# DeltaNet and a SiLU feed-forward in one kernel: where the vector engine makes the weight sums for the last chunk

## The chip, the cores and the metric

The kernel runs on one core of a Trainium2 chip. A core has five engines with a queue each: TensorE (PE in the profile; its weight loads are listed as PEld), VectorE (DVE), ScalarE (ACT), GpSimd (POOL) and SyncE (SP), which here issues DMAs. Each engine works through its own list of instructions in order, and waits on semaphores for the others. Matrix products land in PSUM; ACT and DVE read them from there. The metric is the device time of one execution in microseconds (us), as the median of several.

## What is computed

A DeltaNet layer runs over 4 batches x 8 heads of 768 tokens with 48 features, token by token; its output goes through a feed-forward layer.

```python
for t in range(S):                       # S = 768, state is (B, H, 48, 48)
    y[:, :, t] = einsum('bhd,bhde->bhe', q[:, :, t], state)
    v_old = einsum('bhde,bhd->bhe', state, kt)          # kt: key, normalised
    state = state + bt * einsum('bhd,bhe->bhde', kt, vt - v_old)
x = y.transpose(0, 2, 1, 3).reshape(3072, 384)
h = x @ w_in                             # 384 -> 2048
g = h * sigmoid(h)
out = g @ w_out                          # 2048 -> 384
```

## The kernel before

The 768 tokens are cut into six chunks of 128 (`NCH` = 6), numbered 0 to 5. Inside a chunk the recurrence becomes triangular systems, solved by merging inverted blocks of 32 into 64, and by two halves of 64 tokens (`hf`) that follow one another through the state. Two groups of batches (`g`) go side by side. For a chunk `c`, `solve(c)` is a generator whose steps are, in order: first merge (`merge(c, g, False)`), keys of the first half (`keys(c, g, 0)`), second merge (`merge(c, g, True)`), inner products and old state of the first half (`inner` into `pz`, `old` into `pyc`), state update and new outputs (`made`: `update` into `pu`, `new`), copies (`copy_out`), keys of the second half, inner products of the second half, then its outputs.

`keys` matters here. PE multiplies keys with the state (line 893, into `ph`), and DVE then adds `ph` to the values `vf` (line 898). `inner` (line 905) is PE's next use of that `vf`. Each engine's list is in the order in which the program writes it, since `pin` ties every instruction behind the one before it on its engine. So a DVE instruction that is written earlier stands in front of the `vf` add in DVE's queue, whatever PE waits for.

The feed-forward of an earlier chunk runs between the steps of the solve: the outer loop calls `go(solving)` for one step of the solve and `run(n)` for `n` pieces of the feed-forward. While chunk 5 is solved, the pieces are those of chunk 4: its second layer, `combine(4, hf)`, whose products go to `px` and `py` (line 1451), whose sums of activations are made on DVE (`sum_g`, line 1428), and whose results ACT copies out of PSUM (`kept`, line 1459) for DVE to add to `o` (line 1462).

The first layer for the last chunk, `hidden_by_chains(5)`, runs after that, with fewer products and more sums. It takes combinations of the blocks of `w_in` as weights, which `sum_weights()` makes on DVE: eighteen instructions over 128 x 512 elements, in tiles that the profile calls `w_in`, `sums_of_w_in` and `kb` (lines 1285 and 1280). `weight_sums` is that generator, and `go(weight_sums, n)` writes its next `n` instructions. `BY_CHAINS` is `(5,)`, so this happens only in the loop's pass for chunk 5.

Of the kernel before, what the change touches and what calls it, by code (L numbers as in the profile page):

```python
# [19 lines left out]
def kernel(  # L20
# [85 lines left out]
    def go(steps, n=1):  # L106
        for _ in range(n):
            next(steps, None)

    def together(*parts):  # L110
        for _ in zip_longest(*parts):
            pass
# [82 lines left out]
    def in_blocks(c):  # L195

        return 1 < c < NCH
# [446 lines left out]
    def block_in(c, by_scalar=False):  # L644
        there, g, _ = blocks[c]
        issue(g, there[:], by_scalar)
# [242 lines left out]
    def keys(c, g, hf):  # L889

        ph = bank(CC, "ph")
        for u, p, e, n, of, _ in of_heads():
            yield pin(nc.tensor.matmul(  # L893
                ph[on(e, hf, g), n * D : (n + 1) * D], lhsT=kqs[c, g * HB + u][of, p, 0, on(e, hf, g)],
                rhs=states[g][of, u, p, 0:D], start=True, stop=True,
            ))
        to = vfs[c][:, hf, g * HB : (g + 1) * HB]
        pin(nc.vector.tensor_tensor(out=to, in0=to, in1=by_heads(ph), op=ALU.add))

    def inner(c, g, hf, room=CC):  # L900

        pz = bank(room, "pz")
        for u, p, e, n, _, _ in of_heads():
            rows = on(e, hf, g)
            yield pin(nc.tensor.matmul(  # L905
                pz[rows, n * D : (n + 1) * D], lhsT=xis[g][rows, u * H + 2 * p + e, :],
                rhs=vfs[c][rows, hf, g * HB + u, p, :], start=True, stop=True,
            ))
        to = z_of(g)[:, :, hf]
        if c == 0 and hf == 0:  # L910
            by = (by_act, by_dve) if g == 0 else (by_dve, by_act)
            at = slab[:, g * HB * NP * 2 * D + D :][:, 0 : HB * NP * 2 * D]
            by[0](at.rearrange("p (n w) -> p n w", w=2 * D)[:, :, 0:D], pz[:, 0:DM].rearrange("p (n d) -> p n d", d=D))
            by[1](to, by_heads(pz))
        else:
            by_act(to, by_heads(pz))

    def update(c, g, hf):

        if c == NCH - 1 and hf == 1:  # L920
            return
        pu = bank(CC, "pu")
        for u, p, e, n, to, _ in of_heads():
            rows = on(e, hf, g)
            yield pin(nc.tensor.matmul(  # L925
                pu[to, n * D : (n + 1) * D], lhsT=by_pair(kbufs[c % 2], g)[rows, u, p, e],
                rhs=z_of(g)[rows, u, hf, p], start=True, stop=True,
            ))
        for e in range(2):
            of = slice(W * e, W * e + D)  # L930
            to = states[g][of]
            pin(nc.vector.tensor_tensor(out=to, in0=to, in1=by_heads(pu[of]), op=ALU.add))  # L932
# [7 lines left out]
    def first_outputs(g):  # L940

        pys = [bank(A, f"py{e}") for e in range(2)]
        for u in range(HB):
            for a in range(NKT):
                for n in range(2):
                    for half in range(2):
                        f = P * a + W * half
                        h = f // D + n
                        p, e = h // 2, h % 2
                        at = ((g * HB + u) * NP + p) * 2 * D + D + f - D * h  # L950
                        pin(nc.tensor.matmul(
                            pys[e][HALVES[half], C * a + W * u : C * a + W * (u + 1)],
                            lhsT=slab[on(e, 0, g), at : at + W], rhs=aps[0, g][1][on(e, 0, g), u, h, :],
                            start=True, stop=True,
                        ))
        xT, half = x_half(0, g, 0)
        to = xT[:, :, half]
        even, odd = (py[:, 0 : NKT * C].rearrange("p (a t) -> p a t", a=NKT) for py in pys)
        by_act(to, even)
        pin(nc.vector.tensor_tensor(out=to, in0=to, in1=odd, op=ALU.add))  # L960
# [3 lines left out]
    def move():  # L964
        for to, of in moves:
            in_line(nc.sync.dma_start(out=to, in_=of))
        moves.clear()

    def old(c, g, hf):

        py = pys[g] = bank(A, "pyc")
        for u, p, e, _, of, to in of_heads():
            yield pin(nc.tensor.matmul(  # L973
                py[to, C * p + W * u : C * p + W * (u + 1)],
                lhsT=states[g][of, u, p, 0:D], rhs=kqs[c, g * HB + u][of, p, 1, on(e, hf, g)],
                start=p == 0 and u == 0, stop=False, skip_group_check=True,
            ))
        if hf != g:
            by_act(read[0:D], py[0:D, 0 : 512 : W])
# [45 lines left out]
    def copy_out():  # L1025
        together(copies.pop(0))
# [14 lines left out]
    def solve(c):  # L1041

        if c == 0:
            together(inner(0, 0, 0, CC))
            together(inner(0, 1, 0, M))
            yield
            first_outputs(0)
            yield
            first_outputs(1)
            yield  # L1050
            together(update(0, 0, 0), update(0, 1, 0))
            yield
            together(keys(0, 0, 1), keys(0, 1, 1))
            yield
            together(inner(0, 0, 1), old(0, 0, 1))
            yield
            together(inner(0, 1, 1), old(0, 1, 1))
            yield
            together(update(0, 0, 1), update(0, 1, 1))
            yield  # L1060
            together(new(0, 0, 1), new(0, 1, 1))
            move()
            copy_out()
            copy_out()
            block_in(1, True)
            yield
            return
        together(merge(c, 0, False), merge(c, 1, False))
        if c > 1 and in_blocks(c + 1):
            load_blocks(k, c + 1, G0)  # L1070
        yield
        together(keys(c, 0, 0), keys(c, 1, 0))
        yield
        together(merge(c, 0, True), merge(c, 1, True))
        yield
        for hf in range(2):
            if hf == 1:
                together(keys(c, 0, 1), keys(c, 1, 1))
                if c > 1 and in_blocks(c + 1):
                    turn_all(c + 1, 0, G0)  # L1080
                    load_blocks(q, c + 1, G1)
                    turn_all(c + 1, 0, G1)
                yield
            for g in range(2):
                together(inner(c, g, hf), old(c, g, hf))
            if hf == 1 and c > 1 and in_blocks(c + 1):
                turn_all(c + 1, 1, G0)
            yield
            made(c, hf)
            yield  # L1090
            copy_out()
            if hf == 0:
                yield
# [145 lines left out]
    BY_CHAINS = (NCH - 1,)  # L1239
# [664 lines left out]
    weight_sums = sum_weights()  # L1904
# [44 lines left out]

    for c in range(2, NCH):  # L1950
        solving, more = solve(c), c + 1 < NCH
        for n in range(8):
            go(solving)
            run((1, 1, 2, 2, 1, 1, 2, 2)[n] if c == 2 else (2, 2, 2, 2, 1, 1, 2, 2)[n])
            if n == 2 and c > 2 and more:
                assert done[0] >= start(c) - OUTPUT - 4
                load_blocks(k, c + 1, G1)
            if n == 3 and c > 2 and more:
                load_blocks(q, c + 1, G0)
            if n > 0:  # L1960
                go(after, 8)
            if c in BY_CHAINS:
                go(weight_sums, 2)
        go(after, 99)
        go(solving)
        run()
        if c in BY_CHAINS:
            go(weight_sums, 99)
        assert next(solving, 0) == 0
        if c == 2:  # L1970
            pieces = chained(pieces, *(feed_forward(c) for c in range(2, NCH)))
        if not more:
            break
        run(1 if c == 2 else 2)
        step = block_steps(c + 1)
        ready = prepare(c + 1)
        go(ready)
        run()
        go(ready)
        go(sums_in)  # L1980
        go(sums_in)
        linked(load_v, c + 1)
        load_k(c + 2)
        run_to(start(c))
        paced(invert(c + 1, step), 7 if c == 2 else 4)
        after = lengths(c + 2) if c + 2 < NCH else iter(())
        run_to(start(c) + ITEMS + 3)
        for g in range(2):
            size(c + 1, g)
        for n in range(3 if c == 2 else 2):  # L1990
            go(after, 2 - n)
            run()
        go(after, 1)
# [31 lines left out]
```

## Time and profile before

| | us |
|---|---|
| median of 3 runs | 626.46 |
| the runs | 625.25, 626.46, 627.69 |
| the profiled execution | 627.13 |
| its span, first to last instruction | 625.4 |
| PE busy in it | 607.6 |
| DVE busy in it | 464.5 |
| PE idle at pz, waiting for DVE's add to vf | 1.27 |
| PE idle in its other waits for DVE | 1.2 (pl, line 798), 1.2 (px, line 871), 0.4 (pl, line 782), 0.2 (blocks) |

A row of the timeline has the start from the beginning of the span, the length, the engine, the line of the kernel, the operation, `out<-in` by the program's names, the shape, how many instructions of this kind ran in a row, and in brackets how long the engine was idle before them and which instruction ended the wait. Rows on one engine may overlap by some hundredths, since an instruction's end is recorded later than the next one's start. Rows with "q" behind the engine's name are its instruction queue. The windows view gives busy time by engine in a stretch, and the TensorE clock that was granted there as a share of the full one. Groups by line give busy time and, behind the comma, the mean in ns of one instruction.

### The profile page before, as it was taken

How to read it: one execution, taken by the hardware profiler on the slowest of the kernel's cores; microseconds unless marked ns; L12 is line 12 of the kernel's file. 1: busy time of each engine (PE TensorE's matmuls, PEld its weight loads, DVE VectorE, ACT ScalarE, POOL GpSimd, SP SyncE). 2: the span in 40 equal slices, each digit the busy share in tenths (PEclk: the TensorE clock that was granted, in tenths of full speed). 3: DMA queues.
4: the chain of work that ended last, by engine and by line, in shares of the span. 5: the costliest groups of instructions: out<-in, count | busy, mean ns of one | idle time of the engine just before them, and what ended most of it. 6: DMA issues, size and time to landing. Idle time of an engine off the chain costs nothing.

```text
span 625.4 us, 21910 instructions
## 1 busy us (share of the span) xinstructions
PE 607.6 (97%) x9554; PEld 532.3 (85%) x9554; DVE 464.5 (74%) x983; ACT 247.5 (40%) x562; POOL 82.2 (13%) x83
## 2 busy tenths in 40 slices
PE   8889899999999999999999999999999999999997
PEld 5688788666789988898898998899998899988997
DVE  5865688998978976779976868976869967544632
ACT  3566556142351133533424433424433414435310
POOL 5443620247000010000010000010000010000000
PEclk9959899999999999999999999999999999999999
DMA  7755654155425582236083445084351060110011
GB/s 154 179 120 167 200 135 109 51 153 125 107 54 124 99 146 51 64 81 120 0 155 87 101 93 106 2 155 105 88 103 39 1 112 17 39 25 1 2 25 26
DMA packets 143935, 55.06 MB, mean 88 GB/s; under 512 B 113488, under 2 KB 137296, under 8 KB 143840
## 3 DMA queue, kind: packets, MB, share of 16 engines
q1 hardware_dynamic: 143360, 53.00, 37.9%
q8 instruction: 75, 1.23, 0.8%
q10 hardware_dynamic: 480, 0.67, 0.4%
q14 instruction: 20, 0.16, 0.1%
HBM read 40.99 MB, written 10.49 MB: 82 GB/s over the span
## 4 chain that ended last, share of the span: by engine, by line
PE 53%; DVE 2%; DMA 1%; ACT 1%; issue 1%; SPq 0%; DVEq 0%; ACTq 0%
PE px L1451 12%; PE py L1451 10%; PE hu L1168 9%; PE hx L1168 8%; PE hx L1335 3%; PE hu L1335 3%; PE pa L585 2%; PE pz L905 1%; PE pyc L986 1%; PE pyc L973 1%; PE ph L893 1%; PE pu L925 1%; PE py L847 1%; DMA xe<-low 1%; PE px L847 1%
## 5 line engine op out<-in xcount | busy, mean ns | idle before, releaser
L1114 PE MATMUL phid<-xT,w_in 128*128 128x256 f32 x384 | 90.7, 390 | 0.0
L1114 PEld LDWEIGHTS phid<-xT,w_in 128*128 128x128 f32 x384 | 72.1, 193 | 10.6 <-issue 0.5
L1451 PE MATMUL py<-w_out,sums_of_g 128*128 128x192 f32 x320 | 57.3, 329 | 0.5 <-issue 0.5
L1451 PE MATMUL px<-sums_of_w,sums_of_g 128*128 128x192 f32 x320 | 57.2, 330 | 0.0
L1451 PEld LDWEIGHTS py<-w_out,sums_of_g 128*128 128x128 f32 x320 | 52.2, 190 | 1.2 <-issue 0.6
L1451 PEld LDWEIGHTS px<-sums_of_w,sums_of_g 128*128 128x128 f32 x320 | 52.1, 190 | 1.0 <-issue 0.5
L688 DVE SCALAR_TENSOR_TENSOR rank<-g,step,x 128x31 f32<-128x31 f32 (+15 forms) x124 | 49.7, 400 | 3.7 <-DMA g<-blocks 0.7
L693 DVE TENSOR_TENSOR x<-x,rank 128x31 f32<-128x31 f32 (+15 forms) x124 | 42.4, 342 | 4.4
L521 POOL TENSOR_TENSOR vf<-vf,n_slot 128x768 f32<-128x768 f32 x10 | 14.6, 1475 | 190.0 <-DVE sums_of_g L1428 146.9
L1428 DVE TENSOR_TENSOR sums_of_g<-gT 128x512 f32<-128x512 f32 (+2 forms) x44 | 27.7, 663 | 12.8 <-PE py L1451 12.5
L1462 DVE TENSOR_TENSOR o<-o,kept 128x192 f32<-128x192 f32 (+1 forms) x29 | 12.4, 426 | 33.0 <-ACT kept L1459 33.0
L1168 PE MATMUL hx<-xT,w_in 128*128 128x256 f32 x144 | 36.0, 379 | 0.0
L600 ACT COPY gT<-hu 128x512 f32<-128x512 f32 x36 | 21.1, 586 | 32.9 <-PE hu L1168 22.9
L1168 PE MATMUL hu<-xT,w_in 128*128 128x256 f32 x144 | 34.0, 379 | 0.0
L600 ACT COPY xT<-pyc 48x128 f32<-48x128 f32 (+2 forms) x120 | 31.2, 260 | 1.6
L932 DVE TENSOR_TENSOR state<-state,pu 48x384 f32<-48x384 f32 x44 | 24.3, 553 | 8.6 <-PE pu L925 7.5
L1168 PEld LDWEIGHTS hu<-xT,w_in 128*128 128x128 f32 x144 | 27.4, 190 | 3.7
L1168 PEld LDWEIGHTS hx<-xT,w_in 128*128 128x128 f32 x144 | 27.3, 190 | 3.6
L905 PEld LDWEIGHTS pz<-vf,xi 64*64 64x64 f32 x768 | 25.2, 142 | 4.5 <-issue 2.6
L1451 PE MATMUL py<-w_out,gT 128*128 128x192 f32 x160 | 29.0, 331 | 0.0
L1122 ACT ACTIVATE gT<-phid 128x512 f32<-128x512 f32 x24 | 14.4, 598 | 36.3 <-PE phid L1114 35.7
L1451 PE MATMUL px<-sums_of_w,gT 128*128 128x192 f32 x160 | 28.5, 329 | 0.0
(264 smaller groups left out, 1243.9 us busy)
## 6 DMA issues: line engine op xcount, KB each, us to landing
vf<-in_v_dram SPq DMA_DIRECT2D x48, 96.0 KB, 2.7
out_dram<-o SPq DMA_DIRECT2D x42, 96.0 KB, 2.2
w_out<-in_moe_w_in_dram SPq DMA_DIRECT2D x12, 256.0 KB, 3.0
sums_of_w<-in_moe_w_out_dram SPq DMA_DIRECT2D x8, 384.0 KB, 3.5
blocks<-ap SPq DMA_DIRECT2D x40, 64.0 KB, 2.0
g<-blocks SPq DMA_DIRECT2D x4, 512.0 KB, 3.5
up<-x SPq DMA_DIRECT2D x4, 512.0 KB, 3.1
xi<-up SPq DMA_DIRECT2D x16, 128.0 KB, 3.5
```

The costliest lines, as they stand in the source:

```text
L521: done = pin(nc.gpsimd.tensor_tensor(out=vf, in0=vf, in1=of, op=ALU.mult))
L600: return pin(nc.scalar.copy(to, of))
L688: pin(nc.vector.scalar_tensor_tensor(out=tv, in0=g[:, 0:m, m : m + 1].to_broadcast([P, m, n]), scalar=step[:, m : m + 1], in1=x[:, m : m + ...
L693: yield pin(nc.vector.tensor_tensor(out=x[:, 0:m, m:T], in0=x[:, 0:m, m:T], in1=tv, op=ALU.add))
L905: yield pin(nc.tensor.matmul(pz[rows, n * D : (n + 1) * D], lhsT=xis[g][rows, u * H + 2 * p + e, :], rhs=vfs[c][rows, hf, g * HB + u, p, : ...
L932: pin(nc.vector.tensor_tensor(out=to, in0=to, in1=by_heads(pu[of]), op=ALU.add))
L1114: pin(nc.tensor.matmul(ph[:, j * GT : (j + 1) * GT], lhsT=w_in[:, a, (2 * f + j) * P : (2 * f + j + 1) * P], rhs=xTs[c, hf][:, a, :], star ...
L1122: pin(nc.scalar.activation(out=hidden_of(c, hf, f), in_=ph[:], func=ACTF.Silu, scale=0.5))
L1168: pin(nc.tensor.matmul(to[:, GT * i : GT * (i + 1)], lhsT=weights[:, f], rhs=moving, start=start and i == 0, stop=True, skip_group_check=True,
L1335: pin(nc.tensor.matmul(to[:, GT * i : GT * (i + 1)], lhsT=weights[:, 2 * u + i], rhs=moving, start=start and i == 0, stop=True, skip_group ...
L1428: pin(nc.vector.tensor_tensor(out=sums_of_g[:, k, fs], in0=of[0], in1=of[1], op=op))
L1451: pin(nc.tensor.matmul(to, lhsT=at, rhs=quarter(f, *b) if isinstance(b, tuple) else sums_of_w[b][:, f], start=start and n == 0, stop=n == ...
```

## The change

The same eighteen instructions are written at three places instead of nine. Before: two behind each of the steps 0 to 7 of the loop (behind the solve's step, the feed-forward pieces and the other work of that step), and the rest at the end; with eighteen in all, two are left for the end. After: six ahead of step 0, four at the end of step 2, eight at the end of step 5.

```diff
     for c in range(2, NCH):
         solving, more = solve(c), c + 1 < NCH
+        if c in BY_CHAINS:
+            go(weight_sums, 6)
         for n in range(8):
             go(solving)
             run((1, 1, 2, 2, 1, 1, 2, 2)[n] if c == 2 else (2, 2, 2, 2, 1, 1, 2, 2)[n])
...
             if n > 0:
                 go(after, 8)
             if c in BY_CHAINS:
-                go(weight_sums, 2)
+                go(weight_sums, {2: 4, 5: 8}.get(n, 0))
         go(after, 99)
         go(solving)
         run()
-        if c in BY_CHAINS:
-            go(weight_sums, 99)
         assert next(solving, 0) == 0
         if c == 2:
             pieces = chained(pieces, *(feed_forward(c) for c in range(2, NCH)))
         if not more:
+            assert next(weight_sums, 0) == 0
             break
```

Only DVE's order changes; the lists of PE, ACT, POOL and SP are the same. Three pieces of DVE's list show it. The first is around chunk 5's first merge and first keys; `y` is the merge's copy out of PSUM, and the rows with `w_in` or `sums_of_w_in` as output are weight sums. Before:

```order
L1428 TENSOR_TENSOR sums_of_g<-sums_of_g,gT 128x512 x2
L603 COPY y<-py 32x512 x2
L1428 TENSOR_TENSOR sums_of_g<-gT 128x512 x2
L1285 TENSOR_TENSOR w_in<-w_in 128x4x128 x2
L898 TENSOR_TENSOR vf<-vf,ph 128x384 x2
```

With the change:

```order
L1428 TENSOR_TENSOR sums_of_g<-sums_of_g,gT 128x512 x2
L1285 TENSOR_TENSOR w_in<-w_in 128x4x128 x2
L1285 TENSOR_TENSOR sums_of_w_in<-w_in 128x512
L1285 TENSOR_TENSOR w_in<-w_in 128x4x128
L1285 TENSOR_TENSOR sums_of_w_in<-w_in 128x512 x2
L603 COPY y<-py 32x512 x2
L1428 TENSOR_TENSOR sums_of_g<-gT 128x512 x2
L898 TENSOR_TENSOR vf<-vf,ph 128x384 x2
```

Six sums now stand ahead of the `y` copy, and none between it and the first half's `vf` add. The second piece is DVE's list from the second merge's copy (`xi`) to the state adds. Before:

```order
L603 COPY xi<-px 32x16x32 x2
L1462 TENSOR_TENSOR o<-o,kept 128x192
L1285 TENSOR_TENSOR sums_of_w_in<-w_in 128x512 x2
L1462 TENSOR_TENSOR o<-o,kept 128x384
L1428 TENSOR_TENSOR sums_of_g<-gT 128x512 x2
L1285 TENSOR_TENSOR w_in<-w_in 128x4x128 x2
L932 TENSOR_TENSOR state_93<-state_93,pu 48x384 x2
```

With the change:

```order
L603 COPY xi<-px 32x16x32 x2
L1462 TENSOR_TENSOR o<-o,kept 128x192
L1285 TENSOR_TENSOR w_in<-w_in 128x4x128 x2
L1285 TENSOR_TENSOR sums_of_w_in<-w_in 128x512
L1280 SCALAR_TENSOR_TENSOR sums_of_w_in<-w_in,sums_of_w_in 128x512
L1462 TENSOR_TENSOR o<-o,kept 128x384
L1428 TENSOR_TENSOR sums_of_g<-gT 128x512 x2
L932 TENSOR_TENSOR state_93<-state_93,pu 48x384 x2
```

Four sums instead of two stand between the two adds to `o`, and the two ahead of the state adds are gone. The third piece is DVE's list behind the state adds, around the `vf` add for the second half. Before:

```order
L1462 TENSOR_TENSOR o<-o,kept 128x192
L1285 TENSOR_TENSOR sums_of_w_in<-w_in 128x512
L1280 SCALAR_TENSOR_TENSOR sums_of_w_in<-w_in,sums_of_w_in 128x512
L1428 TENSOR_TENSOR sums_of_g<-sums_of_g,gT 128x512 x2
L1285 TENSOR_TENSOR sums_of_w_in<-w_in 128x512
L1280 SCALAR_TENSOR_TENSOR kb_77<-w_in,sums_of_w_in 128x512
L898 TENSOR_TENSOR vf<-vf,ph 128x384 x2
L1280 SCALAR_TENSOR_TENSOR kb_77<-kb_77,w_in 128x512
L1285 TENSOR_TENSOR sums_of_w_in<-w_in,sums_of_w_in 128x512
```

With the change:

```order
L1462 TENSOR_TENSOR o<-o,kept 128x192
L1428 TENSOR_TENSOR sums_of_g<-sums_of_g,gT 128x512 x2
L1285 TENSOR_TENSOR sums_of_w_in<-w_in 128x512
L1280 SCALAR_TENSOR_TENSOR kb_77<-w_in,sums_of_w_in 128x512
L1280 SCALAR_TENSOR_TENSOR kb_77<-kb_77,w_in 128x512
L1285 TENSOR_TENSOR sums_of_w_in<-w_in,sums_of_w_in 128x512
L1285 TENSOR_TENSOR w_in<-w_in 128x4x128
L1280 SCALAR_TENSOR_TENSOR w_in<-sums_of_w_in,w_in 128x4x128
L1285 TENSOR_TENSOR w_in<-sums_of_w_in,w_in 128x4x128
L1285 TENSOR_TENSOR w_in<-w_in 128x4x128
L898 TENSOR_TENSOR vf<-vf,ph 128x384 x2
```

Of the sums behind the add to `o`, two have moved away to the second piece, and the six that followed the `vf` add now stand in front of it, so that eight do.

## The prediction

> **What bounds the kernel now.** I read the page first, then the timeline around the moved instructions, then the chain of waits, and the windows view for the granted clock.
>
> ```profile
> span 625.4 us, 21910 instructions
> PE 607.6 (97%) x9554; PEld 532.3 (85%) x9554; DVE 464.5 (74%) x983; ACT 247.5 (40%) x562; POOL 82.2 (13%) x83
> ```
>
> TensorE is the bound: 97% busy. DVE has a quarter of the span free, so moving DVE work matters only where PE waits for DVE. The change moves eighteen DVE instructions, between 502 and 537 us of the span. Here is what DVE and its neighbours do in the first part of that stretch (timeline; the brackets give the idle time before a row and what ended it):
>
> ```profile
> 501.76 1.29 DVE L1428 TENSOR_TENSOR sums_of_g<-sums_of_g,gT 128x512 f32<-128x512 f32 x2
> 503.18 2.91 POOL L521 TENSOR_TENSOR vf<-vf,n_slot 128x768 f32<-128x768 f32 x2 [50.43 <-DVE sums_of_g L1428]
> 507.49 1.40 DVE L603 COPY y<-py 32x512 f32<-32x512 f32 x2 [4.44 <-PE py L847]
> 511.48 1.02 DVE L898 TENSOR_TENSOR vf<-vf,ph 128x384 f32<-128x384 f32 x2
> 514.02 0.21 PE L847 MATMUL px<-xi,y 32*32 32x32 f32 x1
> 517.54 1.29 DVE L1285 TENSOR_TENSOR sums_of_w_in<-w_in 128x512 f32<-128x512 f32 x2
> 522.01 0.56 DVE L1462 TENSOR_TENSOR o<-o,kept 128x384 f32<-128x384 f32 x1 [3.18 <-ACT kept L1459]
> 523.69 1.41 DVE L1285 TENSOR_TENSOR w_in<-w_in 128x512 f32<-128x512 f32 x2
> 525.13 2.30 DVE L932 TENSOR_TENSOR state<-state,pu 48x384 f32<-48x384 f32 x4
> ```
>
> DVE has two holes, 4.44 us before the y copy and 3.18 us before the add at 522.01. The second part holds the one place where PE waits for DVE:
>
> ```profile
> 527.39 1.22 PE L893 MATMUL ph<-state,kq 48*64 48x48 f32 x64
> 527.46 0.33 ACT L1459 ACTIVATE kept<-py 128x192 f32<-128x192 f32 x1
> 527.83 0.36 DVE L1462 TENSOR_TENSOR o<-o,kept 128x192 f32<-128x192 f32 x1 [0.39 <-ACT kept L1459]
> 528.10 0.69 DVE L1285 TENSOR_TENSOR sums_of_w_in<-w_in 128x512 f32<-128x512 f32 x1
> 529.43 1.29 DVE L1428 TENSOR_TENSOR sums_of_g<-sums_of_g,gT 128x512 f32<-128x512 f32 x2
> 529.95 1.46 PE L1451 MATMUL px<-sums_of_w,gT 128*128 128x192 f32 x8
> 530.64 0.68 DVE L1285 TENSOR_TENSOR sums_of_w_in<-w_in 128x512 f32<-128x512 f32 x1
> 531.36 0.69 DVE L1280 SCALAR_TENSOR_TENSOR kb<-w_in,sums_of_w_in 128x512 f32<-128x512 f32 x1
> 532.08 1.02 DVE L898 TENSOR_TENSOR vf<-vf,ph 128x384 f32<-128x384 f32 x2
> 532.69 0.25 PE L905 MATMUL pz<-vf,xi 64*64 64x48 f32 x1 [1.27 <-DVE vf L898]
> 533.02 0.69 DVE L1280 SCALAR_TENSOR_TENSOR kb<-kb,w_in 128x512 f32<-128x512 f32 x1
> 536.14 0.69 DVE L1285 TENSOR_TENSOR w_in<-w_in 128x512 f32<-128x512 f32 x1
> 540.14 1.29 DVE L1428 TENSOR_TENSOR sums_of_g<-gT 128x512 f32<-128x512 f32 x2 [3.30 <-PE py L1451]
> ```
>
> PE finishes the px products at 532.69 - 1.27 = 531.42 and waits for the vf add (L898). The keys that feed this add had left PE at 528.6, but the add stood in DVE's queue behind four weight sums. From the start of the add to pz: 0.61 us.
>
> **Part one, six sums ahead of the y copy: nothing.** DVE starts its next instruction 0.60 us after an independent one (533.02 to 536.14 is four steps of 0.60 and one of 0.72) and 0.72 after one it depends on (530.64 to 531.36). Six sums with two dependent steps take 4 x 0.60 + 2 x 0.72 = 3.84 us. They begin where the hole begins, near 502.96, and end by 506.9, 0.6 before the y copy can start. Cover: the hole. If POOL's work at 503.18 slowed DVE one for one they would end 2.9 later, at 509.8, and the copy be 2.3 late; merge two reads y at 514.02, so that too is free. The POOL work itself is released by the instruction before the sums. The two sums that stood before the first vf add go: it starts at about 511.36 instead of 511.48, and PE uses it only after 518. Nothing.
>
> **Part two, four sums behind the xi copy: nothing.** They start at 517.54 and take about 2.7, to 520.2; the hole ends at 522.01. The pair at 523.69 is gone from ahead of the state adds, which so start near 523.84 instead of 525.13. PE took up the keys at 527.39 directly behind its other work, while the last state add ended at 527.43; at most 0.07 us were lost there, and a lead at this point ends in the next wait anyway. Bounds 0 to -0.07 on PE, and 0 on the end.
>
> **Part three, eight sums in one block ahead of the second vf add: +2.51 us.** The block's start is still held by ACT's kept copy (527.46) and the add at 527.83. The two sums between 528.10 and 529.43 are gone: 1.33 saved. sums_of_g starts at 528.10, takes 1.21 up to the next start, so the block starts at 529.31. Its eight steps: 0.72 (into kb), 0.72 (kb onto itself), 4 x 0.60, 0.72, and 0.72 from the last sum to the vf add, which is what 531.36 to 532.08 took. Sum 5.28: the add starts at 534.59, 2.51 later than 532.08. PE has nothing else: pz is next in its order. So the wait grows from 1.27 to 3.78 us and pz starts at 535.20. Bounds: 2.3 (steps of 0.69 where I took 0.72, and the wait on its own result costing nothing) to 2.7 (a wait of 0.1 on each of the two sums_of_g that now wait for DVE). Nothing catches this up. DVE used to run six sums between 533.02 and 536.83 and then idle 3.30 for PE; now it idles the whole time, and everything behind starts from PE's pz.
>
> **Part four, what the longer wait does to the clock: +1.3 us.** The granted TensorE clock falls to a half in two places of this trace (columns: PE busy, PEld, DVE, ACT, POOL, clock, DMA share, GB/s):
>
> ```profile
> 24.53:27.95 3.42, 2.75 (x170) 1.96 (x162) 3.38 (x3) 2.93 (x6) 3.42 (x4) 1.00 0.64 123
> 65.49:68.91 3.42, 2.52 (x122) 2.21 (x122) 2.57 (x5) 3.06 (x6) 3.16 (x4) 1.00 0.54 182
> 68.91:72.32 3.41, 3.41 (x9) 2.67 (x9) 3.29 (x6) 1.53 (x2) 2.81 (x3) 0.50 0.68 213
> 72.32:75.73 3.41, 3.41 (x72) 2.52 (x73) 1.20 (x3) 1.24 (x3) 2.90 (x3) 1.00 0.70 208
> 531.40:534.70 3.30, 2.03 (x130) 1.96 (x129) 3.27 (x6) 0.53 (x2) 0.00 (x0) 1.00 0.50 119
> ```
> ```profile
> 24.21 0.90 PE L585 MATMUL pa<-kq 48*64 48x64 f32 x48
> 25.04 0.91 PE L381 MATMUL pw<-state,ident 128*128 128x384 f32 x2
> 26.32 1.32 PE L782 MATMUL pl<-sums_of_w,ap 32*32 32x16 f32 x128 [0.36 <-DVE sums_of_w L757]
> 65.58 1.07 PE L871 MATMUL px<-xi,xe_y 32*32 32x32 f32 x56
> 66.58 0.90 PE L925 MATMUL pu<-z,kb 64*48 64x48 f32 x53
> 68.38 0.38 PE L925 MATMUL pu<-z,kb 64*48 64x48 f32 x11 [0.90 <-issue]
> 68.68 4.54 PE L1114 MATMUL phid<-xT,w_in 128*128 128x256 f32 x12
> 73.78 1.56 PE L1114 MATMUL phid<-xT,w_in 128*128 128x256 f32 x6
> ```
>
> The clock was down for one window of 3.41 us, behind a window in which PE was 2.52 busy, but with small tiles. So I count what a window streamed in full-array columns: rows/128 x columns/128 x moving columns. The window 65.49 to 68.91: 56 x 2 + 64 x 9 + one phid of 256 = 944, and the clock fell. The window 24.53 to 27.95: 2 x 384 + some 30 pa of 12 + 128 x 1, about 1,250, and it stayed. The limit lies between.
>
> After the change PE is empty for 3.78 us. Ahead of that run dense products, 8 x 192 columns in 1.30 us by a row of the chain of waits, 1,180 a us; behind it 64 pz of 12 and 64 pyc of 9 columns, 1,344 in 2.07 us, 650 a us (chain, then the groups of 531.4 to 537.5 by line):
>
> ```profile
> 536.26 1.30 PE py L1451 x8
> ...
> L905 PE MATMUL pz<-vf,xi 64*64 64x48 f32 x64 | 2.1, 219 | 1.3 <-DVE vf L898 1.3
> L973 PE MATMUL pyc<-kq,state 48*48 48x64 f32 x64 | 2.0, 217 | 0.0
> ```
>
> A window streams under 944 when it starts between 0.80 before and 0.37 + 1.45 behind the start of the empty stretch: 2.62 of 3.41 positions, 77%. With 1,250 as the limit 1.06 + 0.37 + 1.92 = 3.35, 98%. The window's position relative to the kernel I take as open in each execution. Before the change the poorest window holds 1.27 empty, all 1,344 small columns and some dense ones, over 1,400: no fall, as the row at 531.40 shows (1.00). The price: twelve phid took 4.54 where two sixes take 2 x 1.56 = 3.12, 1.42 lost in 3.41. The half-clock window begins between 534.0 and 536.7, so in part it still covers the empty stretch, 0.26 us on average: (3.41 - 0.26) x 1.42/3.41 = 1.3. Bounds 1.0 (the earliest position) and 1.7 (half of 3.41); 0 where the clock does not fall, a case of its own below.
>
> The Trainium skill, "TensorE: Matmul & The Clock Gate", section on the HAM clock gate, has the clock halve after an idle window of about 3.4 us that runs freely, and come back after a busy one. The length agrees with the 3.41 us here; that the window must be idle does not, since the clock fell here after one that was 2.52 of 3.42 busy. By the page's wording an empty 3.78 us holds an idle window in about one position of ten (0.37 of 3.41), and the sum would mostly be the stall alone.
>
> **Sum.** 0 + 0 + 2.51 + 1.3 = +3.8 us. The profiled execution took 627.13 with a span of 625.4; so 630.9 for it, 629.2 of span. The median of the three runs is 626.46 (625.25 to 627.69), 0.67 under the profiled one: **630.3 us**.
>
> **Rivals.**
> - *The stall alone* (0.20): the clock stays. For it: up to 23% of positions, and the limit rests on two windows. 626.46 + 2.51 = 629.0. By the rule of the Trainium skill's page named above, this would be the likelier case.
> - *Two windows at half clock* (0.07): the small tiles behind the stall, streamed at half speed, leave the next window poor as well. Against it: the small tiles alone bring 1,344 columns, and dense products follow them. 630.3 + 1.4 = 631.7.
> - *Not slower: the block starts early* (0.03). Place: ACT's kept copy at 527.46. PE put eight dense products (1.30) between the copy's source and the keys at 527.39, so the source was ready near 526.1; if the copy came then, the block and the vf add would be 1.4 earlier, the stall 2.4 instead of 3.78, and the clock would mostly hold: 626.46 + 1.1 = 627.6. It decides when the copy starts before 527.0. Against it: ACT has the same order, and copies xT up to 527.4.
> - *The change does not do what it says* (0.02): with the third group behind the vf add, as "behind the second half's keys" may be read, the add would start at 529.3 and the wait of 1.27 vanish: 625.2. The listed order has all eight ahead of the add.
>
> **How the numbers follow.** The forecast (stall and one fall of the clock) has 0.68. What a measurement of this kernel can tell from no change is about 0.5%, 3.13 us. The forecast's 3.8 with the spread of the runs (1.2 to each side) is over that in about three of four cases: 0.51; of the stall alone one in five: 0.04; two windows: 0.07; slower 0.64 with a little for sums I sized too small. Faster 0.02, within 0.5% 0.34. The range goes from 628.0 (629.0 less most of the spread) to 632.0 (630.3 with the clock at 1.7 and the spread, and the two windows).
>
> **What would show it.** In the changed profile: DVE's block from about 529.3 to 534.6 in one piece; pz waiting some 3.8 us for vf L898; the holes before 507 and 522 filled and no new PE wait ahead of 531; the clock at 0.50 in one window of 3.41 us that begins behind 534, with px or py of 192 columns slower in it. A pz wait under 2 us, or PE waiting anywhere for y or xi, would make the working wrong; a clock of 1.00 through 531 to 545 leaves the stall alone.

## The result, and the profile after

| | median us | runs | ratio to before, 95% interval |
|---|---|---|---|
| before | 626.66 (624.47 to 629.40) | 10 | |
| changed | 631.59 (628.11 to 633.18) | 10 | 1.0074, 1.0048 to 1.0099 |
| before, beside the later runs | 629.24 (625.46 to 634.91) | 35 | |
| changed, beside them | 632.18 (627.96 to 637.14) | 12 | 1.0047, 1.0017 to 1.0078 |

The change makes the kernel slower: 4.93 us in the first comparison of medians, 2.94 in the second. The prediction had +3.8 and a time of 630.3. The ratios are not quotients of these medians, and differ from them by up to 0.001. One of the 35 runs, 634.91, is a slow one, and neither the ratio nor what is said below of 34 runs has it. From the page of the changed kernel, its span and first row of busy times:

```profile
span 630.1 us, 21910 instructions
...
PE 608.3 (97%) x9554; PEld 533.5 (85%) x9554; DVE 467.5 (74%) x983; ACT 247.3 (39%) x562; POOL 82.9 (13%) x83
```

TensorE's busy time is 0.7 us longer, and the span 4.7. That is not how the loss divides, though: ahead of the moved sums, up to 506 us, this execution happened to be 1.4 us less busy than the one before the change in the same time (491.87 against 493.31). Behind that point the busy time grows by 2.2 us and the idle time by 2.6. The place is the one that was foreseen. The timeline of the changed kernel at the third group, with the two rows of PE that frame it:

```profile
527.33 1.15 PE L893 MATMUL ph<-state,kq 48*64 48x48 f32 x64
...
527.75 0.36 DVE L1462 TENSOR_TENSOR o<-o,kept 128x192 f32<-128x192 f32 x1 [1.69 <-ACT kept L1459]
528.03 1.28 DVE L1428 TENSOR_TENSOR sums_of_g<-sums_of_g,gT 128x512 f32<-128x512 f32 x2
529.24 0.68 DVE L1285 TENSOR_TENSOR sums_of_w_in<-w_in 128x512 f32<-128x512 f32 x1
...
533.81 0.69 DVE L1285 TENSOR_TENSOR w_in<-w_in 128x512 f32<-128x512 f32 x1
534.53 1.02 DVE L898 TENSOR_TENSOR vf<-vf,ph 128x384 f32<-128x384 f32 x2
535.14 0.34 PE L905 MATMUL pz<-vf,xi 64*64 64x48 f32 x1 [3.87 <-DVE vf L898]
538.74 2.23 PE L1451 MATMUL px<-sums_of_w,gT 128*128 128x192 f32 x8
544.84 1.29 DVE L1428 TENSOR_TENSOR sums_of_g<-gT 128x512 f32<-128x512 f32 x2 [9.29 <-PE py L1451]
```

The block runs from 529.24 to 534.5 and the add starts at 534.53; pz waits 3.87 us where it waited 1.27. DVE is then idle for 9.29 us, because what it does next hangs on PE. The px products behind the small tiles take 2.23 for eight. In the kernel before the same eight took 1.57:

```profile
534.69 1.57 PE L1451 MATMUL px<-sums_of_w,gT 128*128 128x192 f32 x8
```

The windows view of the changed kernel tells why (columns as in the prediction: PE, PEld, DVE, ACT, POOL, granted clock, DMA):

```profile
526.46:529.87 3.41, 3.41 (x79) 3.13 (x78) 2.12 (x4) 2.76 (x11) 0.00 (x0) 1.00 0.22 54
529.87:533.29 3.42, 1.41 (x9) 1.11 (x7) 3.35 (x7) 0.00 (x0) 0.00 (x0) 1.00 0.51 121
533.29:536.70 3.41, 1.55 (x60) 1.56 (x63) 2.20 (x4) 0.00 (x0) 0.00 (x0) 0.50 0.01 3
536.70:540.11 3.41, 3.41 (x84) 3.31 (x79) 0.00 (x0) 1.01 (x3) 0.00 (x0) 0.50 0.02 5
540.11:543.52 3.41, 3.41 (x79) 3.11 (x79) 0.00 (x0) 0.61 (x2) 0.00 (x0) 1.00 0.00 0
```

The clock fell to a half, but for two windows, not for one. To see where the time is, I take the starts of four products of PE from each timeline: the second half's keys (L893), pz (L905), the new outputs (pyc, L986), and the first product of the last first layer (L1335).

| kernel | keys to pz | pz to pyc | pyc to L1335 | half-clock windows behind pz's wait |
|---|---|---|---|---|
| before | 5.29 | 4.80 | 12.85 | 0 |
| changed, first profile | 7.81 | 7.05 | 12.84 | 2 |

The rest of the chain, from L1335 to the last product, is 71.14 and 71.13 us, and the stretch from the first merge to the keys 21.26 and 21.27. The first interval holds the wait, and the second holds products that had the clock at 1.00 before the change. So this execution lost 2.52 us in the wait and 2.25 in the clock, 4.77 in all, and nothing anywhere else behind the first merge.

The first group looks different from what I had written, though. DVE and POOL rows of the changed kernel:

```profile
502.89 2.57 DVE L1285 TENSOR_TENSOR w_in<-w_in 128x512 f32<-128x512 f32 x2
505.38 1.96 DVE L1285 TENSOR_TENSOR sums_of_w_in<-w_in 128x512 f32<-128x512 f32 x1
507.37 0.69 DVE L1285 TENSOR_TENSOR w_in<-w_in 128x512 f32<-128x512 f32 x1
508.10 1.29 DVE L1285 TENSOR_TENSOR sums_of_w_in<-w_in 128x512 f32<-128x512 f32 x2
509.43 1.39 DVE L603 COPY y<-py 32x512 f32<-32x512 f32 x2
...
512.18 1.02 DVE L898 TENSOR_TENSOR vf<-vf,ph 128x384 f32<-128x384 f32 x2
```
```profile
503.11 3.68 POOL L521 TENSOR_TENSOR vf<-vf,n_slot 128x768 f32<-128x768 f32 x2 [50.44 <-DVE sums_of_g L1428]
```

The first three sums take 4.5 us from start to start where 2.0 were reckoned, as long as POOL works; POOL's two instructions take 3.68 instead of 2.91. The y copy is 1.94 late (509.43 against 507.49). PE has no wait in this stretch. The second group fills its hole:

```profile
518.80 0.69 DVE L1285 TENSOR_TENSOR sums_of_w_in<-w_in 128x512 f32<-128x512 f32 x1
519.52 0.69 DVE L1280 SCALAR_TENSOR_TENSOR sums_of_w_in<-w_in,sums_of_w_in 128x512 f32<-128x512 f32 x1
521.94 0.56 DVE L1462 TENSOR_TENSOR o<-o,kept 128x384 f32<-128x384 f32 x1 [1.73 <-ACT kept L1459]
```

Of the 3.18 us of idle time before this add, 1.73 are left, and the add still starts when ACT's copy lets it.

### The profile page after: what moved, and what is told of

It reads as the page before. It is cut to its first block, busy times and chain, and to the rows that moved or that the text cites. A ratio compares the mean times of both kernels' runs of the same rounds, so it can differ in the third digit from the quotient of the medians.

```text
span 630.1 us, 21910 instructions
## 1 busy us (share of the span) xinstructions
PE 608.3 (97%) x9554; PEld 533.5 (85%) x9554; DVE 467.5 (74%) x983; ACT 247.3 (39%) x562; POOL 82.9 (13%) x83
## 4 chain that ended last, share of the span: by engine, by line
PE 53%; DVE 3%; DMA 1%; issue 1%; ACT 1%; SPq 0%; DVEq 0%; ACTq 0%
PE px L1451 12%; PE py L1451 10%; PE hu L1168 9%; PE hx L1168 8%; PE hx L1335 3%; PE hu L1335 3%; PE pa L585 2%; PE pyc L973 1%; PE pz L905 1%; PE pyc L986 1%; PE ph L893 1%; PE pu L925 1%; PE py L847 1%; PE px L847 1%; DMA xe<-low 1%
## 5 line engine op out<-in xcount | busy, mean ns | idle before, releaser
L1114 PE MATMUL phid<-xT,w_in 128*128 128x256 f32 x384 | 88.9, 385 | 0.0
L905 PEld LDWEIGHTS pz<-vf,xi 64*64 64x64 f32 x768 | 26.8, 149 | 7.4 <-DVE vf L898 4.2
L905 PE MATMUL pz<-vf,xi 64*64 64x48 f32 x768 | 28.5, 233 | 4.0 <-DVE vf L898 3.9
```

The source lines that it names most:

```text
L905: yield pin(nc.tensor.matmul(pz[rows, n * D : (n + 1) * D], lhsT=xis[g][rows, u * H + 2 * p + e, :], rhs=vfs[c][rows, hf, g * HB + u, p, : ...
L1114: pin(nc.tensor.matmul(ph[:, j * GT : (j + 1) * GT], lhsT=w_in[:, a, (2 * f + j) * P : (2 * f + j + 1) * P], rhs=xTs[c, hf][:, a, :], star ...
```

## The experiments

Theory A: the loss is pz's longer wait for the vf add, and the fall of the clock that this wait brings. Against it stood that the other groups cost something, that the clock falls there anyway, and, within A, that the clock goes by idle time rather than by streamed columns. Each group of kernels was timed beside the kernel before, on the same chip; the times are medians. Where nothing else is said, an edit is made to the changed kernel.

### The block behind the add

```diff
-                go(weight_sums, {2: 4, 5: 8}.get(n, 0))
+                go(weight_sums, {2: 4, 6: 8}.get(n, 0))
```

> The changed kernel with its group of eight written one step later, so that the eight sums stand behind the second half's vf add instead of ahead of it. Theory A (the loss is the wait of pz for vf, and a fall of the clock that this wait brings): vf's add starts at about 529.3, pz waits less than 0.1 us where it waited 1.27 before the change and 3.9 after it, the clock stays at 1.00 there, and the time is 1.27 under the kernel before: about 625.4, ratio 0.998. Theory B (the first two groups cost something, through POOL or the y copy): slower than before by what they cost, 627 to 629. Theory C (the clock falls there for another reason than the wait): the clock falls near 533 here too.

Measured: 626.69 against 628.63, ratio 0.9972 (0.9945 to 0.9999). Its timeline:

```profile
528.18 1.02 DVE L898 TENSOR_TENSOR vf<-vf,ph 128x384 f32<-128x384 f32 x2
529.12 0.68 DVE L1285 TENSOR_TENSOR sums_of_w_in<-w_in 128x512 f32<-128x512 f32 x1
...
537.48 1.29 DVE L1428 TENSOR_TENSOR sums_of_g<-gT 128x512 f32<-128x512 f32 x2 [3.10 <-PE py L1451]
```
```profile
528.64 1.46 PE L1451 MATMUL px<-sums_of_w,gT 128*128 128x192 f32 x8
530.03 0.25 PE L905 MATMUL pz<-vf,xi 64*64 64x48 f32 x1
```

The add is done before PE has finished px, and pz follows without a wait: keys to pz 3.88, which is 1.41 under the kernel before (1.27 of idle time and the rest at its edges). The eight sums then run under PE's work and are over 3.10 us before DVE's next input comes. pz to pyc is 4.80, with the clock at 1.00. Theory A holds; the first two groups are in this kernel too, so they are not what costs, and the clock did not fall there without the wait.

### The wait kept, the clock held up

```diff
         pz = bank(room, "pz")
+        if (c, g, hf) == (NCH - 1, 0, 1):
+            for i in range(9):
+                pin(nc.tensor.matmul(
+                    pz[:, 0:HM], lhsT=gT[:, 1, i % 8, 0:C], rhs=sums_of_w[2][:, i % 8],
+                    start=True, stop=True, skip_group_check=True,
+                ))
         for u, p, e, n, _, _ in of_heads():
```

> The changed kernel with nine extra 128x192 products on TensorE (18 in the profile's count, about 2.93 us at 1.30 for eight) into the pz bank just ahead of pz; pz overwrites what they leave. They need nothing that DVE is late with, so they run inside the wait. Theory A: pz still starts at about 535.1, the clock stays at 1.00, and the time is the stall alone: 626.7 + 2.45 = 629.1, which is 2.4 under the changed kernel. If the second part of the loss is not the clock: 631.6 as the changed kernel, or more.

Measured: 630.01 against 628.63, ratio 1.0015 (0.9988 to 1.0043). PE in it:

```profile
531.56 3.09 PE L905 MATMUL pz<-sums_of_w,gT 128*128 128x192 f32 x18
535.59 0.25 PE L911 MATMUL pz<-vf,xi 64*64 64x48 f32 x1 [0.95 <-DVE vf L898]
```

Keys to pz is 7.82 as in the changed kernel, so the wait is all there, and pz to pyc is 4.80 as before the change: the clock stayed at 1.00. Extra work on the bound engine gave back the second part of the loss. The median difference of 1.4 us is below the 2.5 that the trace shows; the interval (up to 2.7 us) has room for it, but by the times alone this kernel can't be told from the kernel before. That the clock was held is shown by the trace.

### The same filler with small tiles

```diff
+        if (c, g, hf) == (NCH - 1, 0, 1):
+            for i in range(85):
+                pin(nc.tensor.matmul(
+                    pz[0:T, 0:T], lhsT=gT[0:T, 1, i % 8, 0:T], rhs=gT[0:T, 1, i % 8, C : C + T],
+                    start=True, stop=True, skip_group_check=True,
+                ))
```

> As the dense filler, but 85 products of 32x32 tiles (170 in the profile's count, some 17 ns each, 2.9 us): TensorE is busy as long, but streams 340 full-array columns instead of 3,456. If the clock goes by full-array columns (limit between 944 and about 1,250 a window of 3.41 us): it still falls in half to four fifths of the executions, and the median is 630 to 631.6. If it goes by idle time: no window is idle, the clock stays at 1.00 and the time is 629.1 as with the dense filler.

Measured: 635.21 against 628.63, ratio 1.0092 (1.0056 to 1.0127). This run was mis-sized: the tiles took 32 ns each instead of 17, and the filler outlasted the wait (keys to pz 9.37), so its time can't be set against the theories. Its windows say something all the same:

```profile
538.13:541.54 3.41, 3.41 (x122) 3.37 (x121) 1.87 (x4) 0.00 (x0) 0.00 (x0) 1.00 0.02 5
541.54:544.95 3.41, 3.41 (x121) 3.32 (x114) 0.00 (x0) 0.79 (x3) 0.00 (x0) 0.50 0.02 5
```

The profile has TensorE busy without a break from the keys to pz, and the clock fell behind a window that was busy for all of its 3.41 us and streamed 419 full-array columns: there was no wait left for the fall to come from. I cut the filler to 45 products and ran it again:

> The small filler cut to 45 products (90 in the profile's count; they took 32 ns each, not 17, so 2.9 us): it ends inside the wait. Streamed columns: 180. By streamed columns (limit between about 1,100 and 1,430 a window): the clock falls as in the changed kernel, behind a window in which TensorE was hardly idle, and the time is that of the changed kernel, 631 to 632 (ratio 1.005 to 1.008). By idle time: no fall, and the time of the dense filler, 1.5 to 2.5 us above the kernel before.

Measured: 633.23 against 629.24, ratio 1.0061 (1.0029 to 1.0093). The timeline and the windows of this shorter filler:

```profile
531.49 3.03 PE L905 MATMUL pz<-gT 32*32 32x32 f32 x90
535.44 0.34 PE L911 MATMUL pz<-vf,xi 64*64 64x48 f32 x1 [0.92 <-DVE vf L898]
```
```profile
531.10:534.52 3.42, 3.42 (x93) 3.08 (x92) 3.38 (x6) 0.00 (x0) 0.00 (x0) 1.00 0.48 115
534.52:537.93 3.41, 2.49 (x95) 2.50 (x97) 1.29 (x3) 0.48 (x2) 0.00 (x0) 0.50 0.02 5
537.93:541.35 3.42, 3.42 (x51) 3.32 (x46) 0.00 (x0) 0.53 (x2) 0.00 (x0) 0.50 0.03 5
```

In the window from 531.10 PE was busy throughout, 3.42 of 3.42, and the clock fell behind it. Counted in full-array columns it streamed 372, each product counted in the window in which it starts. The kernel with the dense filler was idle as long (0.95 and 0.92) and kept its clock. So idle time, as the profile has it, does not decide, and the work that is streamed does. That the chip counts just these columns is not shown: the last section has windows that they sort wrongly. The ratio of 1.0061 is in the 1.005 to 1.008 expected.

### The block alone, on the kernel before

```diff
-                go(weight_sums, 2)
+                go(weight_sums, {5: 8}.get(n, 2 * (n < 5)))
```

> The kernel before with one part of the change: two sums behind each of the steps 0 to 4 as before, and the last eight in one block behind step 5, ahead of the second half's vf add; the first two groups are not made. Theory A: the add is 6 sums later than before, 3.84 us, pz waits 5.1, the time is 626.7 + 3.84 + about 2.4 for the clock, which falls in every execution: 632.9. Stall alone: 630.5. If moves ahead of it in the changed kernel had cost time rather than given some back: less than the changed kernel's 631.6.

Measured: 633.37 against 628.63, ratio 1.0076 (1.0045 to 1.0107). pz waits 5.1 us, and keys to pz is 9.14, 3.85 over the kernel before where 3.84 was expected. Its windows:

```profile
531.37:534.78 3.41, 0.00 (x0) 0.00 (x0) 3.34 (x7) 0.00 (x0) 0.00 (x0) 1.00 0.24 58
534.78:538.19 3.41, 2.85 (x108) 2.85 (x112) 0.97 (x2) 0.53 (x2) 0.00 (x0) 0.50 0.00 0
538.19:541.60 3.41, 3.41 (x60) 3.13 (x57) 0.00 (x0) 0.97 (x2) 0.00 (x0) 1.00 0.02 5
```

One window without a single product, one at half clock behind it: pz to pyc 6.07, 1.27 lost. 5.12 in the trace, 4.74 in the medians. I had reckoned 2.4 for the clock, as in the first profile of the change, 6.2 in all; here it was one window. That the time came near the expected 632.9 is luck, since the kernel before ran 2 us slower beside these kernels than in the first comparison.

### Four sums ahead, four behind

```diff
-                go(weight_sums, {2: 4, 5: 8}.get(n, 0))
+                go(weight_sums, {2: 4, 5: 4, 6: 4}.get(n, 0))
```

> The changed kernel with its last group cut in two: four sums ahead of the second half's vf add, four behind it. Theory A: the add starts at 529.24 + 0.72 + 0.72 + 0.60 + 0.72 = 532.0, as before the change, so pz waits about 1.2, the clock stays, and the time is that of the kernel before: ratio 1.000. If making the sums in one block were the loss, rather than the wait behind it, some of the 4.9 us would remain.

Measured: 629.73 against 629.24, ratio 0.9998 (0.9967 to 1.0029). pz waits 1.3, keys to pz 5.28, pz to pyc 4.80: the kernel before, to 0.01 us. The block does not cost as a block; how many sums stand ahead of the add does. With none of the eight ahead of it, four, eight, and eight with two more ahead of the sums of g, keys to pz is 3.88, 5.28, 7.81 and 9.14.

### Without the first group

```diff
-        if c in BY_CHAINS:
-            go(weight_sums, 6)
...
-                go(weight_sums, {2: 4, 5: 8}.get(n, 0))
+                go(weight_sums, {0: 2, 1: 2, 2: 6, 6: 8}.get(n, 0))
```

> The kernel with the last eight sums behind the second half's vf add, but without the group ahead of the first merge: two sums behind step 0, two behind step 1 and six behind step 2 instead. None of them runs beside the POOL work on vf. Theory A (the first group is free although POOL stretches it from 3.8 to 6.5 us): the sums run at 0.60 and 0.72 apart, and the time is that of the kernel with the group, 1.3 us under the kernel before. If the first group cost something: faster than that kernel by it.

Measured: 627.24 against 629.24, ratio 0.9955 (0.9929 to 0.9981), the lowest of all. The sums no longer run beside POOL, and keep their pace:

```profile
510.95 1.29 DVE L1285 TENSOR_TENSOR w_in<-w_in 128x512 f32<-128x512 f32 x2
...
520.11 1.42 DVE L1285 TENSOR_TENSOR w_in<-w_in 128x512 f32<-128x512 f32 x2
```

Keys to pz is 3.88 and pz to pyc 4.80, as with the first group. The two kernels with the eight sums behind the add were timed at different times on different chips, and their intervals overlap, so the times do not show that the first group costs nothing. The traces do: between 490 and 531 us TensorE waits for no other engine in either kernel. From the first merge to the keys it is 21.26 us with the group and 22.18 without it. That is no gain of the group: the changed kernel alone, which has it, goes from 21.27 to 22.25 over its five profiles, and the added time is mostly in TensorE's products themselves (the first half's keys alone took 1.52 here and 1.15 there). What stretches them stays open.

### The change again, four more profiles

> The changed kernel itself, beside the other runs of this call, so that its granted clock can be set against that of the kernel before on the same chip. Theory A (wait plus clock): 3.8 to 5 us slower, and the TensorE time lost to the clock, (1 - mean clock) x span, is 1.7 us or more above that of the kernel before; what is left when 0.7 us of time is taken off for each us of lost clock is the wait, about 2.5. Stall alone: the lost clock is the same in both.

Measured: 632.18 against 629.24, ratio 1.0047 (1.0017 to 1.0078). The difference of 2.94 us is under the 3.8 to 5 expected. The clock took (1 - mean clock) x span = 12.7 us on average in its 12 runs and 10.7 in 34 of the kernel before, 2.0 more, as expected. At 0.67 us of time for each (the slope over the 34 runs), that is 1.3 us by the clock; the means of the times differ by 3.3, which leaves 2.0 for the wait, against 2.52 in every trace. The spread of the runs, with a standard deviation of 2.5 us in the lost clock, allows no more exact division.

> The changed kernel once more, one look, for the number of half-clock windows behind the wait (two in both profiles of it so far). Replaying TensorE's products of the kernel before with the longer wait over all positions of the 3.41 us windows, with a limit of 1,100 to 1,430 full-array columns for the fall and 800 to 1,000 for staying down, gives no fall in 0 to 11% of positions, one window in 61 to 87% and two in 2 to 39%. So over three looks: one window (keys to pz 7.8 us, pz to the next pyc of line 986 5.8 to 6.1) at least once. If it is always two (7.0): the limit for staying down is higher than the traces have it, or the windows are tied to the kernel's own start.

> As the look before it, a second draw of the windows' position: one window behind the wait is the likeliest, two are possible, none is rare.

> As the two looks before it, a third draw of the windows' position: one window behind the wait is the likeliest, two are possible, none is rare.

| profile of the changed kernel | keys to pz | pz to pyc | windows |
|---|---|---|---|
| first | 7.81 | 7.05 | 2 |
| again | 7.82 | 7.05 | 2 |
| third (e9) | 7.82 | 6.31 | 1 |
| fourth (e10) | 7.81 | 7.54 | 2 |
| fifth (e11) | 7.82 | 6.10 | 1 |

The wait is the same to 0.01 in all five. The clock fell in all five, and cost 2.25, 2.25, 1.51, 2.74 and 1.30, 2.0 on average, in one window or two by where the 3.41 us windows happened to lie. One window came in two of the last three, as expected. Each of these three ran once, at 637.22, 630.38 and 635.41 us, with 628.89 for the kernel before beside them; single runs spread too far to be compared.

## Why the prediction was right, and where its size was off

**The first two groups, nothing: right, one by its spare cover.** The step "end by 506.9, 0.6 before the y copy can start" was wrong: POOL stretched the six sums from 3.8 us to 6.5. The bound beside it was the one that came true (one for one with POOL's 2.9, copy 2.3 late; measured 2.7 and 1.94), and the cover behind it, merge two at 514, held.

**The third group, +2.51: right.** 2.52 in five profiles, and the same arithmetic gave the other placements: 3.84 reckoned and 3.85 measured for the block alone, none and none for four ahead.

**The clock, +1.3: the mechanism right, the size too small.** The fall came as forecast, behind a window that streamed little, and in five profiles of five. The step that failed is "the half-clock window begins between 534.0 and 536.7", with one window as the rule and two windows at a chance of 0.07. Two things went past it. The limit for the fall was put at 944 to 1,250 columns; in two profiles of the change it fell behind a window with 1,344 (seven px of 192 that start in it). In the first of them the window that began at 533.29 was then at half clock while PE still waited. And I counted the small tiles' 1,344 columns as one sum, enough to bring the clock back; the window boundary cut them, 630 in the window to 536.70, and at half clock they run slower (128 of them from 535.14 to 538.74, 3.6 us where the kernel before had 2.0). So that window was poor as well and the clock stayed down for a second one. In the fourth profile the window began where the prediction had it, 0.86 us ahead of pz, and the 1,008 columns in it still did not bring the clock back, so the cutting of the small tiles is enough for a second window. With one window the cost was 1.27 to 1.51, which is what the term had; with two, 2.25 and 2.74. (The term's lower bound, 1.0, comes to 0.93 by its own numbers: 2.24 us of the window behind the wait at 1.42 lost in 3.41.)

**The sum.** 2.52 + 2.0 = 4.5 by five profiles, against 3.8 forecast, 4.93 and 2.94 in two comparisons of medians. That these lie on either side of 3.8 is in part luck: the clock's share went from 1.30 to 2.74 from one profile to the next, and the medians have a spread of their own. **The stall alone**, which the Trainium skill ("TensorE: Matmul & The Clock Gate", section on the HAM clock gate) would have made the likelier case, did not occur in five profiles; the short filler shows why, with a fall behind a window in which the profile has no idle time. In the third and fifth profile of the change no product starts in the window ahead of the fall, so these two agree with the page as well; in the other three that window was busy for 0.41 to 1.41 us. **The not-slower rivals** are gone: ACT's copy let the add to o start at 527.75, against 527.83 before, and the eight sums stand ahead of the add.

## What to carry to other kernels

An instruction moved into idle time on one engine is free only if it leaves that idle time before the next instruction that the bound engine waits for: count what stands in the queue ahead of that one instruction, and put the rest behind it (here the same eight sums cost 4.5 us ahead of one add and gave 1.4 back behind it). A wait on TensorE should also be priced with what it does to the clock, which tiny products did not keep up here. If a wait can't be removed, dense products that go nowhere are worth trying: in this wait of 3.87 us they kept the clock in the one profile taken and cost no more than the wait itself.

## What the runs showed that I had not expected

- A DVE sum of two 128x512 operands beside POOL's work on 128x768 took two to three times its 0.69 us (two took 2.57, the next 1.96), and POOL's two took 3.68 instead of 2.91. The same sums beside nothing: 1.29 for two. The three sums and POOL's two were through in 4.45 us (502.89 to 507.34), where one behind the other they would need 3 x 0.69 + 2.91 = 4.98: nearly as if they took turns. The Trainium skill ("SBUF — State Buffer", section on its two separate sides) says that a DVE instruction with two inputs in SBUF and a GpSimd instruction that reads SBUF lock each other out of a shared port pair for a whole instruction. These rows nearly bear that out.
- The clock limit in streamed full-array columns is not sharp in these traces. In ten profiles that I counted it fell behind windows with up to 1,432 and stayed behind some with 1,112; under 1,100 it always fell, over 1,500 it never did. Down, it stayed behind up to 987 and came back from 1,000 on. The last three profiles break that second limit: the clock stayed down behind 1,008 in the fourth profile of the change, and in the third behind 1,552 (the window from 18.96). Over all thirteen profiles the best single limit in columns puts 7 windows on the wrong side of fall and no fall, with 37 falls among them; the best limit in TensorE's busy time puts 21. So columns sort better than idle time, but what the chip counts stays open.
- More than half of the spread from run to run goes with this clock: over 34 runs of the kernel before, the time and the clock's loss go together with a correlation of 0.76, 0.67 us for each us. In the profiled execution of the kernel before, all half-clock windows up to the last product lie in the first 75 us, where small tiles run.
